# A step's softmax written behind the second stretch of products and transpositions, from the third batch on

## The chip, the cores and the metric

The kernel runs on one core of one Trainium2 chip. The metric is the device time of one execution in microseconds; the median of the fast runs is quoted. One launch computes everything.

Engines: PE is TensorE (matmuls and transpositions), PEld its weight loads, DVE is VectorE, ACT is ScalarE, POOL is GpSimd, SP is SyncE. L548 is line 548 of the kernel.

## The reference

Attention with a threshold relative to each row's maximum, then a Fourier mix over sequence and features, and a layer of normalization and two products:

```python
scores = scale * (q @ k.T)                      # 8 batches, 8 heads, 576 x 576, head 64
thresh = scores.max(-1) - tau
attn = softmax(where(scores >= thresh, scores, -1e9))
x = heads_joined(attn @ v)                      # 8 x 576 x 512
u = x + real(fft(fft(x, axis=1), axis=2))
un = (u - mean(u)) / sqrt(var(u) + 1e-6)
out = u + relu(un @ w_ch1) @ w_ch2              # 512 -> 2048 -> 512
```

All is float32; `heads_joined` and the normalization of attn are shortened here.

## The kernel before

The work is cut into 160 steps, 20 a batch: a step is 128 query rows of a pair of heads (every fifth has 64). From step 40 on TensorE's order is written by hand, and a scheduler orders the other engines by the place in the program and by its own estimate of when an operand is ready. A step does its scores, its softmax, the transpositions of the softmax of the step before, and then pieces of other work (the Fourier mix of the last batch, the two products of earlier rows), which `fill()` hands out by a budget.

The loop that is changed:

```python
for i in range(2 * per_batch, total + 1):       # steps 40 to 160
    if i < total:
        scores(i)
        softmax(i)

    n, t = divmod(i, NT)
    # ... fold, prep and weights are set up
    next(prep, None)
    fill()                    # first stretch of products
    next(weights, None)       # pe and the first pw of step i - 1
    fill()                    # second stretch
    next(weights, None)       # the second pw
    next(prep, None)
    fill()                    # third stretch
    next(prep, None)
    # ... weighted values, loads, the next batch's mix
```

The softmax, on VectorE and ScalarE:

```python
def softmax(i, between=None, meanwhile=None):
    for j in range(nh):
        nc.vector.tensor_reduce(out=neg[:, j : j + 1], in_=sc[j][...], op=ALU.max, negate=True)   # L461
    for j in range(nh):
        nc.scalar.activation(out=ej, in_=sc[j][...], func=ACT.Exp, bias=neg[:, j : j + 1])        # L469
        if j == 0:
            nc.scalar.activation(out=thr[...], in_=neg[...], func=ACT.Identity, ...)              # L473
        nc.vector.scalar_tensor_tensor(out=ej, in0=sc[j][...], scalar=thr[...], in1=ej,
                                       op0=ALU.is_ge, op1=ALU.mult, accum_out=den[...])           # L477
    # ... 1 / sum (L482, L489), scaling (L492 on VectorE, L496 on ScalarE)
```

And who reads the PSUM banks, the buffers that TensorE writes to and the other engines read. The program lets a tile be written only once the last reader of what its bank held before is done. All tiles of the tag `mm` (pe, pw, py, pa, ph, pn, po, pv, pq ...) share four banks; the score tiles have banks of their own, which one step fills.

```python
pe = ps.tile([128, 4, 128], FP32, tag="mm", bufs=4, name="pe")
nc.tensor.transpose(pe[:, 0, :], e[:, 512:640], ident[:, :])
nc.scalar.copy(ends[...], pe[:, 0, :])                                   # L548, L552
pw = ps.tile([128, 4, 128], FP32, tag="mm", bufs=4, name="pw")
# ... four transpositions
nc.scalar.copy(e_t[...], pw[:, :, :])                                    # L562, L564
# ... in the mix: one bank pa, read twice by VectorE
nc.vector.tensor_tensor(out=low, in0=pa[:, 0:KH], in1=sin, op=ALU.subtract)   # L728
nc.vector.tensor_tensor(out=high, in0=pa[:, 0:KH], in1=sin, op=ALU.add)       # L729
```

Of the kernel before, what the change touches and what calls it, by code (L numbers as in the profile page):

```python
# [28 lines left out]
def _repeated(ap, n):  # L29

    return bass.AP(
        tensor=ap.tensor,
        offset=ap.offset,
        ap=[list(ap.ap[0]), list(ap.ap[1]), [0, n]],
    )
# [12 lines left out]
def kernel(  # L48
# [100 lines left out]
    def load_v(n):  # L149

        b, p = n // NPAIR, PAIRS[n % NPAIR]
        vt = v_in[n % 2]
        for j in range(2):
            h = 2 * p + (j + p) % 2
            nc.sync.dma_start(
                out=vt[:, j:8:2, :], in_=v[b, h, 0:512, :].rearrange("(t p) d -> p t d", p=128)
            )
            nc.sync.dma_start(out=vt[64 * j : 64 * j + 64, 8 + j, :], in_=v[b, h, 512:576, :])
# [230 lines left out]
    def prep_in_parts(n):  # L389


        qk = loaded.pop(n)
        qT = sb.tile([128, S], FP32, tag="qT", name="qT")
        kT = sb.tile([128, S], FP32, tag="kT", name="kT")

        pq = ps.tile([128, 512], FP32, tag="mm", bufs=4, name="pq")
        for t in range(4):
            nc.tensor.transpose(pq[:, 128 * t : 128 * t + 128], qk[:, t, :, :], ident[:, :])
        nc.vector.tensor_scalar(
            out=qT[:, 0:512], in0=pq[:, :], scalar1=q_scale[:, :], scalar2=None, op0=ALU.mult  # L400
        )
        yield
        pk = ps.tile([128, 512], FP32, tag="mm", bufs=4, name="pk")
        for t in range(4):
            nc.tensor.transpose(pk[:, 128 * t : 128 * t + 128], qk[:, 4 + t, :, :], ident[:, :])
        nc.scalar.copy(kT[:, 0:512], pk[:, :])
        yield
        pt = ps.tile([128, 512], FP32, tag="mm", bufs=4, name="pt")
        nc.tensor.transpose(pt[:, 0:128], qk[:, 8, :, :], ident[:, :])
        nc.vector.tensor_scalar(  # L410
            out=qT[:, 512:S], in0=pt[:, 0:64], scalar1=q_scale[:, :], scalar2=None, op0=ALU.mult
        )
        nc.vector.tensor_copy(kT[:, 512:S], pt[:, 64:128])
        heads[n] = (qT, kT, v_in[n % 2])
        if n + 1 < B * NPAIR:
            load_pair(n + 1)

    def normalized(n):


        return n >= 2 * NPAIR

    def scores(i):
        n, t = divmod(i, NT)
        qT, kT = heads[n][0:2]

        nh = 2 if t < 4 else 1
        sc = [ps.tile([128, 2, 512], FP32, tag="sc", name=f"sc{j}") for j in range(nh)]
        if t < 4:
            for c in range(2):  # L430
                for j in range(2):
                    hp = slice(64 * j, 64 * j + 64)
                    nc.tensor.matmul(  # L433
                        sc[j][:, c, 0:HALF], qT[hp, 128 * t : 128 * t + 128],
                        kT[hp, HALF * c : HALF * (c + 1)], start=True, stop=True,
                    )
        else:

            for j, c, c0, k0, w in (
                (0, 0, 0, 0, HALF), (1, 0, 0, 64, HALF), (0, 1, 0, HALF, HALF),  # L440
                (1, 1, 0, 64 + HALF, 512 - HALF), (1, 1, 512 - HALF, 0, 64),
            ):
                hp = slice(64 * j, 64 * j + 64)
                nc.tensor.matmul(  # L444
                    sc[0][hp, c, c0 : c0 + w], qT[hp, 512:S], kT[hp, k0 : k0 + w],
                    start=True, stop=True, skip_group_check=True,
                )
        steps[i] = (sc, nh)

    def softmax(i, between=None, meanwhile=None):  # L450

        t = i % NT
        sc, nh = steps[i]
        neg = sb.tile([128, 2], FP32, tag="neg", bufs=3, name="neg")
        thr = sb.tile([128, 2], FP32, tag="thr", bufs=3, name="thr")
        den = sb.tile([128, 2], FP32, tag="den", bufs=3, name="den")


        e = sb.tile([128, 2 * S], FP32, tag="e", name="e")
        for j in range(nh):  # L460
            nc.vector.tensor_reduce(  # L461
                out=neg[:, j : j + 1], in_=sc[j][:, :, 0:HALF], axis=AXIS_XY, op=ALU.max,
                negate=True,
            )
        if meanwhile is not None:
            meanwhile()
        for j in range(nh):
            ej = e[:, S * j : S * (j + 1)].rearrange("p (c n) -> p c n", c=2)
            nc.scalar.activation(  # L469
                out=ej, in_=sc[j][:, :, 0:HALF], func=ACT.Exp, bias=neg[:, j : j + 1], scale=1.0  # L470
            )
            if j == 0:
                nc.scalar.activation(  # L473
                    out=thr[:, 0:nh], in_=neg[:, 0:nh], func=ACT.Identity,
                    bias=thr_off[:, :], scale=-1.0,
                )
            nc.vector.scalar_tensor_tensor(  # L477
                out=ej, in0=sc[j][:, :, 0:HALF], scalar=thr[:, j : j + 1], in1=ej,
                op0=ALU.is_ge, op1=ALU.mult, accum_out=den[:, j : j + 1],
            )  # L480

            nc.vector.tensor_scalar(  # L482
                out=den[:, j : j + 1], in0=den[:, j : j + 1], scalar1=1e-9, scalar2=None,
                op0=ALU.add,
            )
            if between is not None:
                between()
                between = None
        nc.vector.reciprocal(den[:, 0:nh], den[:, 0:nh])  # L489
        rec = None  # L490
        if normalized(i // NT):
            nc.vector.tensor_scalar(  # L492
                out=e[:, 0:S], in0=e[:, 0:S], scalar1=den[:, 0:1], scalar2=None, op0=ALU.mult
            )
            if nh == 2:
                nc.scalar.activation(  # L496
                    out=e[:, S : 2 * S], in_=e[:, S : 2 * S], func=ACT.Copy, scale=den[:, 1:2]
                )
        else:
            rec = sb.tile([128, 2 * D], FP32, tag="rec", name="rec")  # L500
            nc.gpsimd.tensor_copy(
                rec[:, :].rearrange("p (j d) -> p j d", j=nh), _repeated(den[:, 0:nh], 2 * D // nh)
            )
        if t == 4:
            nc.scalar.copy(e[:, S : S + 64], e[:, 512:S])
        steps[i] = (e, rec)
# [662 lines left out]
    def fill():  # L1169
        nonlocal budget, spent  # L1170
        budget += per_slot
        if mixes:
            mix(1)
        while work and spent < budget and work[0][0] < mixed:
            done = next(work[0][1], None)
            if done is None:
                work.pop(0)
            else:
                spent += done

    total = B * per_batch
# [106 lines left out]
    def fold_more():  # L1288
        if folds and next(folds[0], True):
            folds.pop(0)  # L1290
# [15 lines left out]
    def mix(count):  # L1306
        nonlocal spent, mixed
        for _ in range(count):
            done = next(mixes[0], None)
            if done is None:  # L1310
                mixes.pop(0)
                mixed += 1
                break
            spent += done
# [70 lines left out]
    ctx.enter_context(tc.manual_schedule(engines={mybir.EngineType.PE}))  # L1385

    for i in range(2 * per_batch, total + 1):
        if i < total:
            scores(i)
            softmax(i)  # L1390

        n, t = divmod(i, NT)
        if t > 2:
            fold_more()
        nothing = iter(())
        prep = prep_in_parts(n + 1) if t == 3 and n + 1 < B * NPAIR else nothing
        weights = weights_in_parts(i - 1)
        next(prep, None)
        fill()
        next(weights, None)  # L1400
        fill()
        next(weights, None)
        next(prep, None)
        fill()
        next(prep, None)
        if t == 2:
            weighted_values(n, 0)
        if t == 0:
            while folds:
                fold_more()  # L1410
            weighted_values(n - 1, 1)
            folds.append(fold_rows(n - 1))
            if n % NPAIR == 0:
                while folds:
                    fold_more()
            if n + 1 < B * NPAIR:
                load_v(n + 1)
        if i % per_batch == 0:
            start_batch(i // per_batch - 1)
# [49 lines left out]
```

## Time and profile before

| | before |
|---|---|
| time, median of 3 runs | 1697.56 us (1697.05 to 1699.07) |
| span of the profiled run (a fourth, of 1699.09 us) | 1697.3 us |
| TensorE busy | 1637.6 us, 96% |
| TensorE idle in the changed loop (scores of step 40 to the scores of step 159) | 24.38 us in 55 gaps |
| stretches of half clock (granted clock 0.50) in the loop | 3, of 3.41 us each |

The last two rows come of cutting the trace of TensorE at the start of each step's scores; a gap is a pause of over 0.05 us between the end of one record and the start of the next. The prediction below shows the lines themselves.

One block of lines it doesn't show, which also belongs here, is the order of time on TensorE in step 105 (start, duration, engine, line, tile, then in brackets the idle time before it and what ended it):

```profile
988.28 0.27 PE L541 MATMUL pe<-ident,e 128*128 128x128 f32 x1
989.18 0.66 PE L560 MATMUL pw<-ident,e 128*128 128x128 f32 x4 [0.62 <-ACT ends L552]
990.51 0.41 PE L709 MATMUL pa<-seq_even,y_e 128*1 128x145 f32 x2 [0.68 <-ACT e_t L564]
```

The tile pw doesn't read `ends`. It waits for the copy of `ends` because the bank that it was given is the one pe has just filled. (Building the kernel again shows it: pe and pw of this step both have bank 0.) Keep that in mind.

### The profile page before, as it was taken

The page shows a single profiled execution, that of the slowest core. Times are in us where ns is not written, and L with a number is a line of the kernel's source. Part 1 is how long each engine was busy: PE and PEld are TensorE (multiplying, and loading weights), DVE is VectorE, ACT ScalarE, POOL GpSimd, SP SyncE. Part 2 cuts the span into 40 slices and gives each one's busy share as a digit, 9 for nine tenths or more (in the row PEclk, how much of TensorE's full clock was granted, in tenths as well). Part 3 has the DMA queues.
Part 4 walks back from the last instruction along what each step waited for, and adds up shares of the span by engine and source line. Part 5 has one row for each costly group of instructions (what it writes and reads, how often), then busy time and mean ns, then how long its engine had stood idle before and what let it go on. Part 6 is the DMA issues. An engine that isn't in the chain of part 4 may idle for free.

```text
span 1697.3 us, 28896 instructions
## 1 busy us (share of the span) xinstructions
PE 1637.6 (96%) x10838; PEld 1280.9 (75%) x10838; DVE 1137.2 (67%) x2518; ACT 835.4 (49%) x1817; POOL 585.6 (35%) x779
## 2 busy tenths in 40 slices
PE   8998899999999999999999999999999999999998
PEld 4555555566887787878888778886878778789998
DVE  6885786556757576766566757676676758673454
ACT  5764675543545464645354546454646446442111
POOL 5773463040420442134332143223242144124332
PEclk9999999999999999999999999999999999999999
DMA  5323222010010101000101010100101000000000
GB/s 162 112 54 108 70 73 51 20 33 21 15 38 11 34 15 41 22 27 8 28 22 34 8 34 15 41 22 25 25 15 41 19 24 15 14 1 13 14 14 13
DMA packets 130384, 57.48 MB, mean 34 GB/s; under 512 B 121123, under 2 KB 121125, under 8 KB 130246
## 3 DMA queue, kind: packets, MB, share of 16 engines
q1 hardware_dynamic: 128854, 55.35, 12.1%
q8 instruction: 86, 1.41, 0.3%
q10 hardware_dynamic: 1392, 0.30, 0.1%
q14 instruction: 52, 0.43, 0.1%
HBM read 46.02 MB, written 9.44 MB: 33 GB/s over the span
## 4 chain that ended last, share of the span: by engine, by line
PE 75%; DVE 13%; ACT 8%; issue 2%; POOL 2%; DMA 0%; ACTq 0%; DVEq 0%; POOLq 0%
PE ph L926 23%; PE po L1090 18%; PE pv L589 9%; PE sc L433 7%; PE pw L560 5%; PE po L848 3%; ACT e L469 3%; DVE e L477 3%; DVE neg L461 3%; PE sc L444 2%; PE py L692 1%; PE ph L822 1%; DVE hs L1051 1%; DVE f L673 1%; PE pa L709 1%
## 5 line engine op out<-in xcount | busy, mean ns | idle before, releaser
L461 DVE TENSOR_REDUCE neg<-sc 128x1 f32<-128x576 f32 x288 | 205.7, 750 | 195.2 <-PE sc L433 183.3
L469 ACT ACTIVATE e<-sc,neg 128x576 f32<-128x576 f32 x288 | 212.0, 736 | 248.3 <-DVE neg L461 247.7
L477 DVE SCALAR_TENSOR_TENSOR e<-sc,thr,e 128x576 f32<-128x576 f32 x288 | 227.1, 813 | 59.6 <-ACT thr L473 58.8
L1090 PE MATMUL po<-w,hs 128*128 128x256 f32 x1024 | 248.6, 386 | 0.3 <-DVE u L804 0.3
L1090 PEld LDWEIGHTS po<-w,hs 128*128 128x128 f32 x1024 | 187.5, 192 | 33.3 <-issue 11.0
L926 PE MATMUL ph<-u_t,w 128*128 128x128 f32 x1536 | 187.5, 276 | 0.2 <-ACT u L788 0.2
L560 PE MATMUL pw<-ident,e 128*128 128x128 f32 x1152 | 170.9, 275 | 13.0 <-ACT ends L552 3.2
L926 PEld LDWEIGHTS ph<-u_t,w 128*128 128x128 f32 x1536 | 178.7, 192 | 4.9 <-issue 3.1
L433 PE MATMUL sc<-kT,qT 64*128 64x288 f32 x1024 | 167.0, 430 | 7.0 <-DVE e L477 6.4
L562 ACT COPY e_t<-pw 128x512 f32<-128x512 f32 x256 | 148.4, 593 | 47.3 <-PE pw L560 45.6
L935 DVE TENSOR_TENSOR hs<-ph,hs 128x512 f32<-128x512 f32 x160 | 107.3, 685 | 79.9 <-PE ph L926 56.6
L560 PEld LDWEIGHTS pw<-ident,e 128*128 128x128 f32 x1152 | 135.4, 141 | 32.2 <-issue 4.7
L433 PEld LDWEIGHTS sc<-kT,qT 64*128 64x128 f32 x1024 | 92.0, 186 | 68.4 <-issue 41.4
L926 PE MATMUL ph<-t_u,s_w 128*128 128x128 f32 x1024 | 126.1, 276 | 2.0 <-ACT ends L548 1.1
L804 DVE SCALAR_TENSOR_TENSOR u<-po,rstd,u 128x256 f32<-128x256 f32 (+1 forms) x164 | 76.2, 483 | 77.2 <-PE po L1090 75.4
L926 PEld LDWEIGHTS ph<-t_u,s_w 128*128 128x128 f32 x1024 | 119.3, 192 | 5.9 <-issue 2.3
L1090 PE MATMUL po<-hs,s_tile 128*128 128x256 f32 x512 | 122.0, 382 | 0.0
L943 ACT ACTIVATE hs<-hs 128x512 f32<-128x512 f32 x112 | 69.3, 629 | 70.9 <-DVE hs L935 70.8
L1090 PEld LDWEIGHTS po<-hs,s_tile 128*128 128x128 f32 x512 | 93.6, 190 | 13.6 <-issue 2.1
L496 ACT ACTIVATE e<-e,den 128x576 f32<-128x576 f32 x96 | 74.4, 775 | 53.2 <-DVE den L489 52.6
L1086 POOL TENSOR_TENSOR hs<-hs,s_tile 128x512 f32<-128x512 f32 x32 | 42.2, 1320 | 126.1 <-PE po L1090 120.1
L492 DVE TENSOR_SCALAR e<-e,den 128x576 f32<-128x576 f32 x120 | 81.4, 678 | 2.6
(199 smaller groups left out, 2886.0 us busy)
## 6 DMA issues: line engine op xcount, KB each, us to landing
hs<-in_moe_w_ch_dram SPq DMA_DIRECT2D x23, 512.0 KB, 4.3
out_dram<-u SPq DMA_DIRECT2D x36, 256.0 KB, 2.1
qk_in<-in_q_dram SPq DMA_DIRECT2D x64, 128.0 KB, 2.3
v_in<-in_v_dram SPq DMA_DIRECT2D x64, 128.0 KB, 2.3
qk_in<-in_k_dram SPq DMA_DIRECT2D x31, 128.0 KB, 2.4
w<-in_moe_w_ch_dram SPq DMA_DIRECT2D x6, 512.0 KB, 7.6
qk_in<-in_k_dram SPq DMA_DIRECT2D x31, 64.0 KB, 2.2
stage<-in_moe_w_ch_dram SPq DMA_DIRECT2D x3, 512.0 KB, 3.8
```

Of the source, the lines that this page charges most:

```text
L433: nc.tensor.matmul(sc[j][:, c, 0:HALF], qT[hp, 128 * t : 128 * t + 128], kT[hp, HALF * c : HALF * (c + 1)], start=True, stop=True,)
L461: nc.vector.tensor_reduce(out=neg[:, j : j + 1], in_=sc[j][:, :, 0:HALF], axis=AXIS_XY, op=ALU.max, negate=True,)
L469: nc.scalar.activation(out=ej, in_=sc[j][:, :, 0:HALF], func=ACT.Exp, bias=neg[:, j : j + 1], scale=1.0)
L477: nc.vector.scalar_tensor_tensor(out=ej, in0=sc[j][:, :, 0:HALF], scalar=thr[:, j : j + 1], in1=ej, op0=ALU.is_ge, op1=ALU.mult, accum_out ...
L492: nc.vector.tensor_scalar(out=e[:, 0:S], in0=e[:, 0:S], scalar1=den[:, 0:1], scalar2=None, op0=ALU.mult)
L560: nc.tensor.transpose(pw[:, c, :], e[:, c0 : c0 + 128], ident[:, :])
L562: nc.scalar.copy(e_t[:, 4 * j : 4 * j + 4, qs], pw[:, :, :])
L589: nc.tensor.matmul(pv[64 * j : 64 * j + 64, 0:m], vt[:, 2 * c + j, :], e_t[:, 4 * j + c, 0:m] if c < 4 else ends[:, 0:m], start=(c == 0), ...
L804: nc.vector.scalar_tensor_tensor(out=u, in0=product, scalar=self.rstd[:, t : t + 1], in1=u, op0=ALU.mult, op1=ALU.add,)
L926: nc.tensor.matmul(banks[name][:, 128 * q : 128 * q + 128], left[c][:, 512 * part + 128 * q : 512 * part + 128 * q + 128], right[c], start ...
L935: nc.vector.tensor_tensor(out=to, in0=bank, in1=to if other is None else other, op=ALU.add)
L1090: nc.tensor.matmul(bank[:, 0 : DM // 2], left[p], right[p], start=start and p == 0, stop=p == NK - 1, skip_group_check=True,)
```

## The change

A step's exponentials, maxima and maskings are written behind the first two stretches of products, so that the scheduler puts the copies and sums of those stretches, which free banks for TensorE, ahead of them. The whole diff, blank lines left out:

```diff
     for i in range(2 * per_batch, total + 1):
         if i < total:
             scores(i)
-            softmax(i)
         n, t = divmod(i, NT)
 ...
         fill()
         next(weights, None)
         next(prep, None)
+        if i < total:
+            softmax(i)
         fill()
```

## The prediction

> **What bounds the kernel now.** I read the page first, to see which engine the span belongs to.
>
> ```profile
> span 1697.3 us, 28896 instructions
> PE 1637.6 (96%) x10838; PEld 1280.9 (75%) x10838; DVE 1137.2 (67%) x2518; ACT 835.4 (49%) x1817; POOL 585.6 (35%) x779
> PE   8998899999999999999999999999999999999998
> PE 75%; DVE 13%; ACT 8%; issue 2%; POOL 2%; DMA 0%; ACTq 0%; DVEq 0%; POOLq 0%
> ```
>
> TensorE is busy 96% of the span and carries 75% of the chain that ended last. A change that adds and removes no matmul can win only TensorE's idle time and time in which it runs at a lower clock. The changed loop starts with step 40, whose scores start at 298.70 us, and its last softmax belongs to the scores that end at 1491.0. So the second view is the busy time by stretch, cut there.
>
> ```profile
> core 0: us, PE busy (x) PEld busy (x) DVE busy (x) ACT busy (x) POOL busy (x), PEclk, DMA share, GB/s
> 298.70:1491.00 1192.30, 1167.92 (x8081) 937.62 (x8080) 811.52 (x1824) 604.73 (x1298) 355.75 (x471) 1.00 0.09 24
> ```
>
> 1192.30 - 1167.92 = 24.4 us of idle TensorE in the whole loop, 1.4% of the time before. The idle time before it (298.70 - 270.03 = 28.7 us) and after it (206.30 - 199.64 = 6.7 us) is outside the change. Third, the waits of TensorE in that stretch (waiting line, what ended the wait, us in total, times, longest):
>
> ```profile
> PE py L692 <- ACT ends L548: 5.3, 4, 1.5
> PE pw L560 <- ACT ends L552: 3.2, 4, 1.3
> PE pa L709 <- ACT e_t L564: 2.7, 4, 0.7
> PE pw L560 <- ACT y_e L702: 2.2, 1, 2.2
> PE ph L926 <- ACT u L788: 1.4, 6, 0.2
> PE py L692 <- ACT y_e L702: 1.2, 1, 1.2
> PE py L692 <- DVE f L673: 1.0, 3, 0.3
> ```
>
> Most of it is TensorE waiting for a copy by ScalarE. A py tile does not read `ends`: it waits for the PSUM bank that the copy of `ends` sets free (the `mm` tiles have four). The fourth view shows why such a copy is late: the order of time in step 142.
>
> ```profile
> 1332.35 0.63 ACT L697 COPY y_e<-py 128x256 f32<-128x256 f32 x1 [2.56 <-PE py L692]
> 1333.44 0.33 PE L541 MATMUL pe<-ident,e 128*128 128x128 f32 x1 [0.26 <-DVE u L804]
> 1333.91 1.40 DVE L461 TENSOR_REDUCE neg<-sc 128x1 f32<-128x576 f32 x2
> 1334.75 0.74 ACT L469 ACTIVATE e<-sc,neg 128x576 f32<-128x576 f32 x1 [1.77 <-DVE neg L461]
> 1335.39 0.26 ACT L548 COPY ends<-pe 128x128 f32<-128x128 f32 x1
> 1335.70 1.20 PE L692 MATMUL py<-dim_s,f 128*128 128x128 f32 x4 [1.49 <-ACT ends L548]
> ```
>
> The transposition pe ends at 1333.77. ScalarE is idle then (1.77 us), but next in its order is the exponential of this step, which waits for VectorE's maximum, itself late behind the fold of the Fourier mix. The copy of `ends` stands behind that exponential and TensorE idles 1.49 us. Steps 102, 122 and 142 (at 958.66, 1147.20 and 1334.21 us) are alike.
>
> The last view is the clock around two of these idle times.
>
> ```profile
> 960.28:963.69 3.41, 3.41 (x12) 2.69 (x12) 3.38 (x11) 1.65 (x4) 0.56 (x1) 0.50 0.00 0
> 963.69:967.10 3.41, 3.41 (x27) 2.27 (x28) 1.02 (x1) 1.81 (x4) 0.71 (x1) 1.00 0.00 0
> 1148.69:1152.10 3.41, 3.41 (x22) 2.67 (x22) 3.41 (x9) 2.99 (x7) 1.68 (x1) 1.00 0.00 0
> ```
>
> After the idle time that ended at 960.15 the granted clock is 0.50 for 3.41 us, after the equal one that ended at 1148.69 it stays 1.00. The same drop follows the idle times at 537.2 and 1335.7, so three of them lie in the loop. Each costs about half of 3.41 us: from the late py to the third po after it are 4.19 us in step 102 and 2.52 us in step 122, 1.7 us more. That time counts as busy and comes on top of the 24.4 us.
>
> [...] `ends` ran after the exponential although its input was there for 1.6 us. [...]
>
> **The change part by part.** The diff moves one call, the softmax of a step, from ahead of the first stretch of products to behind the second. PE is ordered by hand, so its order cannot change: the built programs have the same 6313 instructions on it in the same order, and the same 1826, 2232 and 784 on ACT, DVE and POOL. What changes is the order on those engines, which a scheduler sets by place in the program: the copies, sums and folds of the first two stretches now go ahead of the softmax. I compared the built order step by step.
>
> Gains:
> 1. Steps 102, 122, 142. ScalarE's order is now y_e, y_e, ends, e_t, y_o and then the exponential. The 1.49 us go. VectorE has the f folds and the u sums ahead of the maxima, so the wait for f (0.33) and the one for u (0.27) just before should go too: 3 x 2.09 = 6.3 us, and two clock drops, 2 x 1.7 = 3.4 us.
> 2. Step 42: both y_e copies move ahead of the second exponential (0.73 us) but stay behind the first: about 0.7 of 1.15 us.
> 3. Step 62: y_e goes ahead of the exponentials, but `ends` remains behind the first, and on VectorE the maximum now stands behind one more combination (0.68 us). By the durations, `ends` is done near 537.3 while TensorE would want the bank at 535.9: 1.4 of the 2.18 us return one matmul group later. Gain 0.8, and half a chance for the clock drop, 0.85.
> 4. The four u copies (L787, L788) no longer stand on both sides of the exponential: 1.4 us of short waits.
> 5. tmp (L729) now follows L728 at once: 0.5 us.
> Sum: 6.3 + 3.4 + 0.7 + 0.8 + 0.85 + 1.4 + 0.5 = 13.95 us.
>
> Unchanged, because the order there is the same: step 82 (0.86 us), steps 65, 105, 125, 145 (`ends` behind both exponentials, then e_t: 1.34 + 3 x 0.62 + 4 x 0.68 = 5.9), steps 116, 136, 156 (3 x 0.35).
>
> Losses. The softmax now ends later. Before, from the last masking (L477) to the next scores that need the same score banks there are 4.6 us in the median step, but 2.2 to 2.5 us in steps 61, 101, 121, 141. In those, four pieces of the mix go ahead of the maskings: L652 0.78, L804 0.47, L677 0.45, L673 0.52, so 2.2 us, some 2.0 with the overlap that successive rows show. That uses the slack up; L673 took 1.5 us where POOL was busy. I book 0.3 us for four steps, 1.2. In steps 79, 99, 119, 139, 159 the threshold (L473) falls behind two or three ScalarE copies, so L477 holds up VectorE's queue and a later sum that frees a bank (L935) comes some 0.7 us later; booked at 0.4 x 5 = 2.0. For waits I have not found in 120 steps, 1.5. Sum 4.7.
>
> Net 13.95 - 4.7 = 9.2 us: 1697.56 - 9.2 = 1688.3, said as 1688.
>
> **The rivals.** First, a new wait takes the place of the one removed: scores wait for banks that the later masking still holds. Against it stands the median slack of 4.6 us against a shift of one to two; for it, the four short steps and the last steps, where 158 has 1.95 us. If it were general, say 1 us in half of 120 steps, plus clock drops, the time would be above 1750. I give that little. Second, the gain is only shifted: the maximum waits behind the copies, and what was late in one stretch is late in the next (step 62 shows it). Then 3 to 5 us remain, and 1693 to 1695. Third, it all goes well: no new waits and all three clock drops gone, 1683. Fourth, VectorE becomes the bound: at 604.73 (ACT) and 811.52 us (DVE) of 1192.3 neither is near, only in the fold steps for some us.
>
> **Range and chances.** The ceiling is 24.4 us of idle and 3 x 1.7 of clock, 29.5 us or 1.7%, so over 2% faster cannot come from this loop. The range is 1682 (all gains, no losses) to 1695 (the second rival). Faster by over 2%: 0.01. Within 2%: 0.97. Slower by over 2%: 0.02, for a general wait on the score banks.
>
> **What would show it.** In the changed profile py <- ends (L548) should fall from 5.3 to about 0.9 to 2.3 us, u L788 and the 2.2 us of y_e L702 vanish, ends L552 and e_t L564 stay at 5.9 together, and at most one stretch of 0.50 clock remain in the loop. The idle time of TensorE in the loop should go from 24.4 to about 18 us. I am wrong if sc (L433) waits for DVE e (L477) by more than 3 us in the loop, if the low-clock stretches stay three or more, or if PE's busy time at full clock changes.

## The result, and the profile after

The changed kernel takes 1679.88 us (1679.80 to 1680.75, 4 runs) against 1697.41 us (1697.05 to 1699.07) of the kernel before in the same rounds: 17.5 us less, ratio 0.9896 with a 95% interval of 0.9879 to 0.9913, within 2%. Ratios here and below are the mean time of one kernel's fast runs over that of the other's of the same rounds, so not quite the ratio of the medians that are quoted. All runs of this study were in the fast state. The direction and the class were right. The predicted 1688 was 8 us too slow, and the range of 1682 to 1695 missed on the fast side.

The page of the changed kernel:

```profile
span 1678.0 us, 28904 instructions
PE 1626.3 (97%) x10838; PEld 1277.1 (76%) x10838; DVE 1142.1 (68%) x2518; ACT 837.2 (50%) x1817; POOL 581.2 (35%) x779
PE 76%; DVE 15%; ACT 7%; issue 2%; POOL 1%; DVEq 0%; ACTq 0%
```

No engine's count of busy instructions changed, and yet TensorE is busy for 11.3 us less (1637.6 - 1626.3). The matmuls are the same, so the 8.4 us of it that lie in the loop are put down to the clock (3.4 us, an estimate) and to time lost at waits that the records count as busy (5.0 us), both below. The spans differ by 19.3 us, more than the times, because the profiled run before was one of the slower ones; 1.65 us of it lie ahead of step 40 (298.70 against 297.06 us), where nothing was changed. The loop by the busy times of the engines, from the scores of step 40 to the end of those of step 159 (columns as in the prediction's second view):

```profile
297.06:1471.62 1174.56, 1159.52 (x8081) 935.28 (x8080) 816.38 (x1823) 606.60 (x1297) 351.70 (x471) 1.00 0.10 24
```

TensorE's idle time there is now 1174.56 - 1159.52 = 15.0 us, where it was 24.4, and its busy time there is 8.4 us less (1167.92 - 1159.52). The waits of TensorE in this stretch:

```profile
PE py L692 <- ACT ends L548: 3.0, 2, 1.6
PE pv L589 <- ACT e_t L562: 2.4, 3, 0.8
PE ph L926 <- POOL t_u L900: 1.8, 1, 1.8
PE pe L541 <- DVE u L804: 1.5, 3, 0.6
PE pw L560 <- DVE qT L399: 1.5, 3, 0.5
PE ph L926 <- DVE hs L935: 1.2, 4, 0.3
PE pw L560 <- DVE tmp L729: 0.7, 4, 0.2
```

Of the seven lines of before, `ends` L548 is down from 5.3 to 3.0, y_e L702 (2.2) and u L788 (1.4) are gone, as predicted. But `ends` L552 (3.2) and e_t L564 (2.7), which the prediction left at 5.9, are gone too. New is pv behind e_t (2.4), and the one wait for GpSimd grew from 0.6 to 1.8.

Step 142, whose lines before are in the prediction, now runs so (other lines left out):

```profile
1318.47 0.30 PE L541 MATMUL pe<-ident,e 128*128 128x128 f32 x1 [0.59 <-DVE u L804]
1318.80 0.27 ACT L548 COPY ends<-pe 128x128 f32<-128x128 f32 x1 [0.75 <-PE pe L541]
1319.12 0.71 PE L692 MATMUL py<-dim_s,f 128*128 128x128 f32 x4
1321.49 0.74 ACT L469 ACTIVATE e<-sc,neg 128x576 f32<-128x576 f32 x1 [0.96 <-DVE neg L461]
1322.93 0.58 ACT L562 COPY e_t<-pw 128x512 f32<-128x512 f32 x1
1323.57 0.65 PE L589 MATMUL pv<-e_t,v_rev 128*64 128x256 f32 x4 [0.80 <-ACT e_t L562]
```

`ends` is copied the moment pe is done, and py follows without a gap: the 1.49 us are gone. In exchange pe waits 0.59 instead of 0.26 us, and pv waits 0.80 us, because the second e_t copy is the one that stands behind both exponentials now. A part of the wait was handed on.

And step 105, against the lines of before:

```profile
978.80 0.27 PE L541 MATMUL pe<-ident,e 128*128 128x128 f32 x1
979.25 0.63 PE L560 MATMUL pw<-ident,e 128*128 128x128 f32 x4 [0.18 <-DVE tmp L729]
979.81 0.41 PE L709 MATMUL pa<-seq_even,y_e 128*1 128x145 f32 x2
```

pw now waits 0.18 us for VectorE's second sum L729 rather than 0.62 us for `ends`, and pa not at all. The tile has another bank: in the changed kernel's build it is that of the first pa, which L729 reads last.

One stretch of low clock is left in the loop, behind the wait for GpSimd in step 85. In the 3.41 us ahead of it TensorE was busy for 1.59 us:

```profile
753.69:757.10 3.41, 1.59 (x14) 1.41 (x13) 1.18 (x3) 1.26 (x2) 3.41 (x6) 1.00 0.01 2
757.10:760.51 3.41, 3.41 (x18) 3.41 (x18) 1.23 (x2) 0.58 (x1) 3.32 (x7) 0.51 0.00 0
```

How many such stretches an execution has differs from run to run of one kernel (the granted clock of a run was 0.992 to 0.996 before; the last section has the idle time ahead of the stretches of both traces), so the count of a single trace is a sample. Over all runs the mean granted clock was 0.994 before (41 runs with a record of it) and 0.996 after (4 runs); 0.002 of 1690 us are some 3 us, an estimate that agrees with two stretches fewer.

Where the 17.7 us of the loop went (start of step 40 to start of step 159, 1191.12 us before, 1173.38 after): 9.34 us are idle time, 24.38 to 15.04; two stretches of half clock fewer are an estimated 2 x 1.7 = 3.4 us (1.7 from the 4.19 against 2.52 us of steps 102 and 122 before); the remaining 5.0 us go with the count of gaps, which fell from 55 to 35. That is 0.25 us a gap beyond what the gap shows, on average; a step that lost one gap got 0.10 to 0.27 us more than the gap. Step 52 lost a visible gap of 0.23 us and is 0.50 us shorter, step 77 lost 0.23 and is 0.45 shorter. The records of step 116 show where it goes. Without a wait the matmuls of ph last 0.28 us each and start 0.11 us apart, so that each overlaps the one before by 0.17. At the wait this overlap is lost, and the first matmul behind it takes 0.38 us: 0.17 + 0.10 us beside the visible gap of 0.35, and the step became 0.62 shorter when the wait went. By groups of steps, before to after:

| steps | length, us | of it idle, us |
|---|---|---|
| 102, 122, 142 | -6.43 | -2.34 |
| 65, 105, 125, 145 | -5.60 | -5.21 |
| 116, 136, 156 | -1.85 | -1.06 |
| 62 | -1.92 | -0.55 |
| 42 | -0.82 | -0.82 |
| short waits elsewhere (47, 48, 51, 52, 77, 78, 80, 92, 96, 117, 137, 157 and others) | -6.52 | -2.48, with the last row |
| longer: 81, 82, 85 | +3.64 | +2.03 |
| longer: 71 to 73, 111 to 113, 131 to 133, 151 to 153 | +1.07 | +1.09 |
| longer: others | +0.71 | |

### The profile page after: what moved, and what is told of

The parts are those of the page before. It is cut to its first block, busy times and chain, and to the rows that moved or that the text cites. A ratio compares the mean times of both kernels' runs of the same rounds, so it can differ in the third digit from the quotient of the medians.

```text
span 1678.0 us, 28904 instructions
## 1 busy us (share of the span) xinstructions
PE 1626.3 (97%) x10838; PEld 1277.1 (76%) x10838; DVE 1142.1 (68%) x2518; ACT 837.2 (50%) x1817; POOL 581.2 (35%) x779
## 3 DMA queue, kind: packets, MB, share of 16 engines
q8 instruction: 86, 1.41, 0.4%
## 4 chain that ended last, share of the span: by engine, by line
PE 76%; DVE 15%; ACT 7%; issue 2%; POOL 1%; DVEq 0%; ACTq 0%
PE ph L926 24%; PE po L1090 18%; PE pv L589 8%; PE sc L433 7%; PE pw L560 5%; PE po L848 3%; DVE e L477 3%; DVE neg L461 2%; ACT e L469 2%; DVE hs L1051 2%; PE sc L444 2%; PE ph L822 1%; PE py L692 1%; PE pd L112 1%; PE pa L709 1%
## 5 line engine op out<-in xcount | busy, mean ns | idle before, releaser
L935 DVE TENSOR_TENSOR hs<-ph,hs 128x512 f32<-128x512 f32 x160 | 107.0, 685 | 72.1 <-PE ph L926 46.8
L804 DVE SCALAR_TENSOR_TENSOR u<-po,rstd,u 128x256 f32<-128x256 f32 (+1 forms) x164 | 75.5, 484 | 73.8 <-PE po L1090 71.9
L622 POOL TENSOR_TENSOR half<-x 128x287 f32<-128x287 f32 x48 | 40.2, 857 | 126.5 <-ACT x L595 70.7
```

Source lines behind the costliest of these rows:

```text
L804: nc.vector.scalar_tensor_tensor(out=u, in0=product, scalar=self.rstd[:, t : t + 1], in1=u, op0=ALU.mult, op1=ALU.add,)
L935: nc.vector.tensor_tensor(out=to, in0=bank, in1=to if other is None else other, op=ALU.add)
```

## The experiments

Four questions: in which steps does the gain arise, is later simply better, which single order carries it, and can both kernels be beaten. Fifteen kernels ran, all of them correct, in several sets of rounds on different chips. Each is compared with the kernel before in its own rounds; kernels of different sets are compared by these ratios.

### Which steps

mix_steps writes the softmax late only while a Fourier mix is under way when the step starts (five steps of a batch's twenty), other_steps only in the rest.

```diff
     for i in range(2 * per_batch, total + 1):
+        behind = bool(mixes)          # other_steps: not mixes
         if i < total:
             scores(i)
-            softmax(i)
+            if not behind: softmax(i)
 ...
         next(prep, None)
+        if i < total and behind: softmax(i)
         fill()
```

> The softmax is written late only in the five steps of each batch in which the Fourier mix runs, early in the other fifteen. Theory A (a copy that frees a PSUM bank stood behind the softmax, mostly in the mix): the step lengths of the two traces put about 10.8 of the loop's 18 us here, so about 1687 us. Rival B (the gain is spread evenly over the steps, five of twenty): 4.5 us, about 1693. Rival C (only the lost clock drops count): 3.4 us or less, about 1694.

> The complement: late only in the fifteen steps of each batch without the mix. Theory A: the rest, about 7 us, so about 1690, and with the other run it adds up to the whole 17.5 us within 2 us. Rival B: 13 us, about 1684. Rival C: no clock drop is removed here, so about 1697.

Measured, against 1697.62 us (7 runs) of the kernel before in the same rounds: mix_steps 1684.17 us (ratio 0.9923, 0.9907 to 0.9940), other_steps 1691.96 us (0.9964, 0.9944 to 0.9985). So 13.4 us and 5.7 us, in sum 19.1, within the 2 us of 17.5 that were allowed; a quarter of the steps gives seven tenths of the sum. A gain spread evenly over the steps falls. So does one of the clock alone: mix_steps has no stretch of half clock in its loop (the profiled execution's granted clock was 0.997, against 0.992 before), but its idle time also fell from 24.38 to 16.80 us. In mix_steps, steps 65, 105, 125 and 145 are shorter by 5.60 us in sum, just as in the changed kernel, and 116, 136 and 156 by nothing.

### Is later better

behind_first writes the softmax behind the first stretch and the first half of the transpositions, behind_third behind the third stretch.

```diff
         fill()
         next(weights, None)
+        if i < total: softmax(i)      # behind_first
         fill()
         next(weights, None)
         next(prep, None)
         fill()
         next(prep, None)
+        if i < total: softmax(i)      # behind_third
```

> The softmax is written behind the first stretch of products and transpositions, not the second. Theory A: the copies of the first stretch (y_e, ends, the first e_t) are already ahead, so most of the gain of the mix steps is there, about 1684 to 1688. If what counts is the second stretch (the second e_t, tmp, the u copies), about 1693.

> The softmax is written behind the third stretch too. Theory A with the slack as its limit: the shortest steps lose, waits of the scores (L433) for the masking (L477) over 3 us, 1682 to 1692. Rival D (later is simply better, the slack of 3.7 us in the median step is ample): below 1678.

Same rounds as above: behind_first 1683.64 us (0.9917, 0.9902 to 0.9932), behind_third 1688.75 us (0.9949, 0.9934 to 0.9964). By the medians both lie behind the changed kernel, but only behind_third clear of the noise: the interval of behind_first overlaps the changed kernel's (0.9879 to 0.9913). Later isn't simply better. What stops it, in the waits of behind_third:

```profile
PE sc L433 <- DVE e L477: 6.3, 5, 2.0
```

Scores wait for the maskings that still hold the score banks: the first rival of the prediction, which the changed kernel, one stretch earlier, doesn't meet. The chosen place is the best of these three by the medians.

### One order at a time

From here on the softmax stays where the kernel before has it, and single instructions are moved in the scheduler's eyes. `tc.high_priority(offset=150)` makes the scheduler treat an instruction as if it were written 150 places earlier, with -150 later. TensorE's order was the same in all of these builds.

**tmp_first** moves VectorE's two reads of pa alone:

```diff
-            nc.vector.tensor_tensor(out=low, in0=pa[:, 0:KH], in1=sin, op=ALU.subtract)
-            nc.vector.tensor_tensor(out=high, in0=pa[:, 0:KH], in1=sin, op=ALU.add)
+            with ahead(): nc.vector.tensor_tensor(out=low, in0=pa[:, 0:KH], ...)    # L728
+            with ahead(): nc.vector.tensor_tensor(out=high, in0=pa[:, 0:KH], ...)   # L729
```

> Kernel before, softmax where it was, with only the two sums L728/L729 (VectorE reads the bank pa twice) given a higher priority to the scheduler; TensorE's order is the same, and on VectorE the second sum now stands right behind the first and ahead of the two maskings in steps 65, 85, 105, 125, 145. Theory E (the predicted 'unchanged' 5.9 us at steps 105, 125, 145 and at 65 went because VectorE freed the bank pa earlier, not because of anything on ScalarE): the waits pw<-ends L552 and pw<-e_t L564 vanish in those steps, each is 1.2 to 1.9 us shorter, together 4.5 to 6 us: 1691.5 to 1693. Rival F (it took ScalarE's later exponentials as well): the waits stay and the time is 1696 to 1698.

Measured 1692.05 us (9 runs) against 1695.73 (18 runs), ratio 0.9974 (0.9964 to 0.9984). A step by step comparison with before: 65, 105, 125, 145 are shorter by 4.73 us, 104, 124, 144 by 1.41, step 85 is longer by 1.37. Step 142 is shorter by 1.67 and step 122 longer by 1.57, because one stretch of half clock came at 122 instead of 142; it is three stretches in both traces. Nothing else in the loop moves by more than 0.15 us. The waits:

```profile
PE py L692 <- ACT ends L548: 5.3, 4, 1.5
PE pw L560 <- ACT y_e L702: 2.2, 1, 2.2
PE pw L560 <- DVE tmp L729: 1.3, 4, 0.5
```

The first two lines are those of before to the digit; `ends` L552 and e_t L564 are not in the list any more, and pw waits for tmp L729 in their place. So the better part of the 5.9 us that the prediction called unchanged is VectorE's (4.73 us here against 5.60 in the changed kernel; all_by_priority below reaches 5.60): no instruction of the softmax was rewritten and no ScalarE copy favoured. The built programs tell how. In step 125 of the kernel before, pw carries waits on TensorE and ScalarE, here and in the changed kernel on VectorE and TensorE. The build gave pw the bank of pa, free once L729 has read it, in place of the bank of pe. (Built again, pw of step 105 has pe's bank 0 before, and the bank of the first pa here and in the changed kernel, 3 and 2.)

**act_first** moves ScalarE's copies out of the `mm` banks (17 statements: `kT`, `ends`, `e_t`, `x`, `y_e`, `y_o`, `sin`, `u`, `hs`), **copies_first** these and the two sums, **after_copies** does the latter to the changed kernel.

```diff
-                nc.scalar.copy(dst[:, q0 : q0 + 128], pe[:, c, :])
+                with ahead(): nc.scalar.copy(dst[:, q0 : q0 + 128], pe[:, c, :])      # L548
-                nc.scalar.copy(e_t[:, 4 * j : 4 * j + 4, qs], pw[:, :, :])
+                with ahead(): nc.scalar.copy(e_t[:, 4 * j : 4 * j + 4, qs], pw[:, :, :])
 ... likewise the others
```

> Kernel before, softmax where it was, with only ScalarE's copies out of the mm banks given a higher priority (the two sums on VectorE not). TensorE's order is the same. Theory A (a step waited because a copy that frees a bank stood behind the softmax on ScalarE; where the softmax itself stands does not matter): the waits py<-y_e, pn and mm on u L788 and the long ones of steps 102, 122, 142 shrink, 8 to 13 us gained without moving the softmax: 1684 to 1690. Rival G (the exponentials themselves had to be later, because in the scheduler's order they are ready first and still stand in front when the copy becomes ready): under 4 us gained, 1693 to 1698.

> Kernel before with both: ScalarE's copies and VectorE's two sums at higher priority, the softmax written where it was. Theory A with E: the two effects add (they sit at other steps), 13 to 18 us: 1679 to 1685, level with the changed kernel. Rival G: at most the sum of the two single runs, over 1688.

> The changed kernel with the same copies and sums at higher priority as well. Theory A: what is left there of waits for ends L548 (6.6 us in 3), y_e L702 (0.3) and tmp L729 (0.7) shrinks: 1674 to 1679. Rival H (what is left is not a matter of order: the copies start as soon as their products end): 1679 to 1681, the same as the changed kernel.

Same rounds as tmp_first: act_first 1693.57 us (0.9981, 0.9972 to 0.9990), copies_first 1688.76 us (0.9952, 0.9939 to 0.9964), after_copies 1680.63 us (0.9908, 0.9894 to 0.9922). The theory that only the copies must come first, and that it doesn't matter where the softmax stands, fails: 2 to 3 us instead of 8 to 13. (The profiled run of act_first is the fastest of its ten, 1688.62 us at a granted clock of 0.997, without a half-clock stretch in the loop.) The two effects do add. In act_first the waits of steps 102, 122 and 142 keep their 2.08 us of idle. ScalarE in step 102 of act_first:

```profile
953.06 0.74 ACT L469 ACTIVATE e<-sc,neg 128x576 f32<-128x576 f32 x1 [1.77 <-DVE neg L461]
953.70 0.26 ACT L548 COPY ends<-pe 128x128 f32<-128x128 f32 x1
953.85 0.31 ACT L473 ACTIVATE thr<-neg,thr_off 128x2 f32<-128x2 f32 x1
```

The favoured copy still stands behind the exponential. ScalarE sits idle for 1.77 us at the head of its queue, waiting for VectorE's maximum, with a copy behind it whose operand is there. 150 places of priority did not put the copy ahead of the exponential; presumably the scheduler believed the maximum to be ready sooner than the chip has it, which no run here tests. In after_copies the same priorities change nothing that the time shows.

**neg_late** therefore delays VectorE's maxima and nothing else; **neg_early** undoes it in the changed kernel; **neg_late_tmp** joins it with the two sums.

```diff
-            nc.vector.tensor_reduce(
+            with tc.high_priority(offset=-150): nc.vector.tensor_reduce(   # L461; neg_early: after, +150
                 out=neg[:, j : j + 1], in_=sc[j][:, :, 0:HALF], axis=AXIS_XY, op=ALU.max,
```

> Kernel before with one thing: the row maxima L461 on VectorE given a lower priority to the scheduler, everything of the softmax written where it was. In steps 102, 122 and 142 the built order of ScalarE becomes that of the changed kernel (both exponentials behind ends, e_t and y_o); L728/L729 stay as before. Theory I (the exponential's place on ScalarE follows from where the maximum stands on VectorE: ScalarE waited up to 1.8 us for the maximum with a ready copy of ends behind it): the waits py<-ends of 2.08 us of idle a step at 102, 122, 142 vanish, 2.5 us a step or 7 to 8 us with the clock stretches that followed two of them: 1687 to 1690; steps 105, 125, 145 keep their 1.3 us of idle. Rival J (the whole softmax must be late): under 3 us, 1693 to 1697.

> The undoing: the changed kernel with only the row maxima L461 given a higher priority, the rest of the softmax late. In steps 102, 122 and 142 ScalarE's built order is that of the kernel before again. Theory I: the three waits py<-ends of about 1.5 us (2.08 us of idle a step) are back, and with them one or two clock stretches: 5 to 9 us slower than the changed kernel, 1685 to 1689. Rival J: at most 2 us slower, 1680 to 1682.

> Kernel before with the maxima late and the two sums L728/L729 early, exponentials, maskings and the rest written where they were. Theories E and I together: the two gains add, since they are at other steps (102, 122, 142 against 65, 105, 125, 145): 11 to 14 us, 1682 to 1685, most of the change's 17. If they don't add (a wait removed in one place comes back 3 steps later): 1687 or more.

Measured, against 1697.41 us (9 runs): neg_late 1692.44 us (0.9970, 0.9958 to 0.9983), neg_early 1682.54 us (0.9911, 0.9898 to 0.9925), neg_late_tmp 1685.54 us (0.9931, 0.9918 to 0.9945). In neg_late ScalarE's built order at step 102 is that of the changed kernel, and steps 102, 122, 142 are shorter by 5.35 us, the two half-clock stretches included; without these it is about 2.0 us, less than the 7 to 8 with them that was expected. The waits tell why:

```profile
PE pe L541 <- DVE u L804: 2.6, 3, 0.9
PE py L692 <- ACT ends L548: 2.5, 2, 1.6
PE pv L589 <- ACT e_t L562: 2.4, 3, 0.8
```

The three waits of some 1.5 us for `ends` are gone (of the two that remain the longer is at step 62), but in each of the three steps pe now waits 0.9 us for the sums u (L804), and pv 0.8 for e_t. The idle time of a step falls only from 2.08 to between 1.64 and 1.70. The place of the maximum sets the exponential's place, as supposed; the long wait goes, and most of its time comes back in two others. neg_early, from the other side, lengthens the same three steps by 3.70 us in sum and the median by 2.7 (the intervals of the two ratios overlap, so the steps carry this), where 5 to 9 were expected; its py waits for `ends` are back:

```profile
PE py L692 <- ACT ends L548: 6.6, 5, 1.4
```

Maxima and sums together gain 11.9 us, two thirds of the change; in the loops of the traces it is 4.80 and 5.00 apart and 11.24 together, and the excess of 1.44 is no more than the 1.7 us of the half-clock stretch that neg_late has in step 65 and this run doesn't.

### The rest, and a kernel that beats both

**pool_first** is the changed kernel with GpSimd's sums t_u (L900) favoured. **all_by_priority** is neg_late_tmp with ScalarE's copies favoured too, **all_and_pool** that with L900, **after_all** the changed kernel with copies, the two sums and L900 favoured.

```diff
-                nc.gpsimd.tensor_tensor(out=out_[c], in0=in0[c], in1=in1[c], op=ALU.subtract)
+                with ahead(): nc.gpsimd.tensor_tensor(out=out_[c], in0=in0[c], in1=in1[c], op=ALU.subtract)   # L900
```

> The changed kernel with GpSimd's sums L900 (t_u) at higher priority: a try to beat both kernels. The changed kernel has a wait ph<-POOL t_u of 1.81 us once, at step 85, where one sum stands behind four additions L731/L735. If those additions need not come first, the wait shrinks by 0.5 to 1.5 us, and the clock stretch at 757 us (1.7 us lost) may go with it: 1677 to 1679.5. If the last sum is limited by its own inputs (u_t written by the additions): 1679.5 to 1681, the same.

> Kernel before with the softmax's exponentials, maskings and scalings written where they were, and three changes of priority alone: maxima L461 later, sums L728/L729 earlier, ScalarE's copies out of the mm banks earlier. ScalarE's built order at steps 42, 62 and 102 is nearly that of the changed kernel. Theory K (the change's gain is the sum of these three orders: 11.9 of the first two as measured, 3.2 of the copies as measured, a part of it shared): 1681 to 1684. Rival L (what is left to the changed kernel's 1680 comes of the rest of the softmax standing late, as in steps 116, 136, 156, where ScalarE's order is the same in both): the copies add nothing, 1685 to 1687.

> The same with GpSimd's sums L900 earlier as well, a try to beat both kernels. If step 85's wait for t_u (1.99 us of idle in the run with maxima late and sums early) goes: 1 to 3 us less than the run without, 1679 to 1683. If not: the same as it.

> The changed kernel with copies, L728/L729 and L900 at higher priority, the other try. The runs with the copies alone (1680.6) and with L900 alone (1679.8) were level with the changed kernel (1679.9), so 1678 to 1681; under 1677 would mean that they help each other.

Measured: pool_first 1679.84 us (rounds of neg_late; 0.9894, 0.9880 to 0.9907); against 1697.14 us (7 runs) all_by_priority 1684.01 (0.9920, 0.9905 to 0.9934), all_and_pool 1683.65 (0.9920, 0.9905 to 0.9935), after_all 1679.27 (1676.43 to 1679.86; 0.9896, 0.9880 to 0.9913). In pool_first the 1.81 us wait for t_u is down to this:

```profile
PE ph L926 <- POOL t_u L900: 0.4, 1, 0.4
```

and step 85 is 2.63 us shorter, the half-clock stretch gone with it; but step 73 is 0.99 longer (so it is in after_copies, which leaves L900 alone), and the runs don't tell pool_first or after_all from the changed kernel. No kernel tried beats it by a margin that these intervals would show.

all_by_priority settles most of what was open. With the softmax written early, three changes of order give 13.1 us by the medians. What the changed kernel has beyond it is of two kinds. In 116, 136, 156 (1.85 us, idle 0.35 each in all_by_priority as in before), 47 and 48 (1.0 us) and 96 (0.6) the priorities changed next to nothing. In 51, 92, 117, 137 and 157 (3.3 us) they took away the wait for the u copies but put a longer one in its place, which ends with the softmax's den on VectorE (L482, L489; 0.27 to 0.70 us), and the changed kernel has neither. Against that, all_by_priority is 1.6 us ahead in 104, 124 and 144. Writing the softmax late gets what these three orders don't; whether a fourth order would is open. In step 116 ScalarE's order is the same before and after; but on VectorE the second of the two sums u (L804) that read a po bank stands behind both maskings before (1092.22 us) and ahead of them after (1080.15), and the built wait of ph changes from ScalarE to VectorE. That is the pattern of L729 once more; no run moved L804 alone, so there it is argued from the order and not shown.

## Why the prediction was wrong, by its own steps

The intent, the direction, the class and the bottleneck were right, and so was the view that led there: the waits of TensorE for banks. By the groups of steps above, the changes are 23.1 us of gains and 5.4 us of losses, where the prediction had 13.95 and 4.7.

**The step that failed is "Unchanged, because the order there is the same".** It put 65, 105, 125, 145 (5.9 us) and 116, 136, 156 (1.05) at zero. They became 5.60 and 1.85 us shorter: 7.45 us, where the loop as a whole was missed by 8.5. (The other errors, +4.6 for the short waits, +0.4 for gains 2 and 3, -3.3 for gain 1 and -0.7 for the losses, nearly cancel.) The premise was true for ScalarE, and the conclusion false: the order on VectorE had changed, so another bank became free first and the tile was built on that one. The profile's line said "waits for `ends`"; I read it as "this step depends on `ends`", when it said only that this bank happened to be the one of `ends`. tmp_first shows it, 4.73 us with two instructions. The prediction even noted the move of L729 (its gain 5) and booked 0.5 us for it. For 116, 136 and 156 the same is argued and not shown.

**Gain 1**, steps 102, 122, 142: 6.3 us of idle and 3.4 of clock were predicted. The clock came in full in these two traces. Of the idle only 2.34 us went, 6.43 in all with the clock. The order on ScalarE was as said and the 1.49 us did go; but the claim that VectorE now has the u sums ahead of the maxima changed little: they were ahead of them before too (in step 142 they start 2.86 us after the step, the first maximum 4.24). They end only 0.30 us earlier, while TensorE, no longer held up by f, comes 0.54 earlier, so pe waits 0.59 us, not zero. And the second e_t copy moved behind the exponentials (0.80). This is the second rival, a gain that is shifted, in this one group; neg_late, which delays the maxima alone, shows the same shift.

**Gains 2 and 3**, steps 42 and 62: 0.7 and 1.65 us predicted, 0.82 and 1.92 measured. In step 62 the sum was nearer than its parts: 0.55 us of idle went instead of 0.8, and a whole half-clock stretch where half a one was booked, which was luck (all_by_priority, with the same 1.64 us of idle left, has it). The late return at step 62 was also right: its `ends` still makes py wait up to 1.6 us.

**Gains 4 and 5**, short waits: 1.9 us predicted, 6.52 measured in the steps that only had short waits. The six waits for u are gone as said. Gain 5 failed: in steps 104, 124 and 144 pa no longer waits 0.21 us for tmp, but 0.30 us for den (L482). The size was off for two reasons. The six (steps 51, 52, 92, 117, 137, 157) show 0.23 us each and their steps are shorter by 0.5 to 0.57 us, 3.1 in sum; and short waits in steps 47, 48, 77, 78, 80 and 96, some 3.0 us, weren't listed.

**The losses**, 4.7 us, were 5.4, but at other places. Not one is at the score banks in the chosen position, and hs (L935) waits 1.2 us where it waited 0.9, against the 2.0 booked. They are the step 85, 2.59 us with a half-clock stretch behind a 1.81 us wait for GpSimd, and small ones at 71 to 73, 81 and 82 and their like. A sum that comes out right by other parts is luck.

**What would show it**: idle time to about 18 us (it is 15.0), one low-clock stretch (one), `ends` L548 to 0.9 to 2.3 us (3.0), u L788 and y_e 2.2 gone (gone), L552 and L564 unchanged at 5.9 (gone: the sign of the failure), scores behind maskings not over 3 us (none), PE's busy time at full clock unchanged (it fell by 5.0 us, 8.4 less 3.4 of clock: a second sign, which the lost overlap at waits explains). The ceiling of 29.5 us left that overlap out too.

The range followed from the same sum: its fast end, 1682, was "all gains, no losses" (1697.56 - 13.95 gives 1683.6) of a list that held steps worth 7.45 us for unchanged and the short waits at a third of their worth.

## What to carry to other kernels

A wait for a copy that frees a PSUM bank belonged here to a bank, not to an instruction (pw in step 105: 0.62 us for `ends` before, 0.18 us for L729 after): when an order changes on any engine that frees banks, compare the waits that the built program puts on each TensorE tile, not only the order of the engine that the profile names. A ready copy stuck behind an instruction that waited for another engine came free when what that instruction waited for was moved (the maximum on VectorE: in neg_late the three waits of 1.5 us went), though other waits took most of the time back (2.08 us of idle a step became 1.64 to 1.70); favouring the copy left the 2.08 us of those steps (act_first). And many short gaps were worth more than their sum: 0.25 us each on average beyond what they show.

## What the traces show of the clock, the gaps and the banks

- The clock: in the traces of the two kernels (before, after) the stretches of half clock begin whole multiples of 3.413 us apart. With the loops cut into pieces at these multiples, the pieces just ahead of the three stretches before (from 533.61, 956.87 and 1332.33 us) hold 1.99, 1.75 and 1.75 us of visibly idle TensorE, and the one ahead of the one after (from 753.73 us) 1.82 us; none of the other pieces of these two loops has more than 1.55 us (before, from 564.33 us), and no half clock follows those. At step 102 before, 1.49 and 0.27 us fell in one piece; at step 122, with the same waits, two pieces have 1.30 and 0.68 us, and the granted clock stayed 1.00. The other traces don't make a rule of it: in behind_third a piece with 1.05 us was followed by half clock too. The 2.08 us of steps 102, 122 and 142 were followed by half clock in two of three before and in tmp_first (granted clock of the execution 0.992 in both), and in none of three in act_first (0.997); the 1.64 to 1.70 us a step of neg_late (0.995) in none. Each stretch cost about 1.7 us, an estimate from the 4.19 us of step 102 and the 2.52 us of step 122 from the late py to the third po behind it.
- Reading gaps: a wait that shows 0.23 us took 0.45 to 0.50 us of the step (steps 77 and 52); in step 116 matmul records that overlap by 0.17 us without a wait stop overlapping at one; and 20 gaps fewer went with 5.0 us beyond idle time and clock.
- The banks: the build decided which bank a tile of the tag `mm` got, and an order changed on VectorE changed what TensorE waited for: pw in step 105 waited 0.62 us for ScalarE, and after two sums had moved on VectorE 0.17 us for VectorE (tmp_first).
